# The last three expert down-projection slots and their epilogue moved two column halves later in TensorE's stream

## The chip, the cores and the metric

The kernel runs on one core of one Trainium2 chip. The metric is the device time of one execution in microseconds (us). Where it is on record, the mean clock that was granted to TensorE over the run stands beside the time, as a share of full speed.

## The reference, cut to what matters

```python
# x: 2048 x 1024, bf16
g = sigmoid((x * gate_w).sum(-1))
a = ssm(x)                                  # a scan over 2048 steps between two projections
idx = argsort(-(x @ w_r))[:8]               # 8 rows of x
y = (silu(x[idx] @ w_gate) * (x[idx] @ w_up)) @ w_down      # w_down: 3584 x 1024
b = x + scatter_add(idx, y * sigmoid(r[idx]))
out = g * a + (1 - g) * b
```

The long work on TensorE is the two projections of `a`. The expert part works on 8 rows only, but it has to read all of `w_gate`, `w_up` and `w_down` (22 MB in bf16).

## The kernel before

The kernel writes the instruction order of TensorE, VectorE, ScalarE and SyncE itself. The second projection ("S2", with H, the scanned states as VectorE prepares them, as one operand) goes through 16 row tiles `b`, each in two column halves `dh`. One half is 16 matmuls of 128x512. Other work is hung between the halves with `at((block, place), fn)`: it is issued after the first half whose place reaches it. In block 9 the halves are (12,0) at place 0.99, (12,1) at 1.99, (13,0) at 2.99 and (13,1) at 3.99.

Each expert step, a "slot", needs a weight tile of 8 KB per partition. Four tiles exist for the down-projection, and it has seven slots. A slot that has run gives its tile back, and the next load goes into it:

```python
def load_w():
    while nload[0] < NS and free_w:
        s = nload[0]
        tag = free_w.pop(0)
        ...                                     # w_gate, w_up slots cut
        w = const.tile([P, 2, 2, D], BF16, name="wd", tag=tag)
        for i in range(2):
            ...                                 # two items of 512 KB, nc.sync.dma_start(w[...], wd_v[...])
        wq[s] = (w, tag); nload[0] += 1

def moe_slot(s):
    for i in range(2):
        moe_item(2 * s + i, wq[s][0][:, i])     # down-projection: 8 narrow matmuls per item into y4 (PSUM)
    free_w.append(wq.pop(s)[1])
    load_w()
```

The epilogue turns `y4` into an update of 8 rows of the output. The last 256 rows of the output are read back after the scatter:

```python
def fin_a():        # ScalarE: 4 evictions of y4 to yc
def fin_b():        # VectorE: yc * rsel * (1 - g)
def scatter_upd():  # GpSimd: scatter-add of yc to out; SyncE: reload of the last rows, tile ul
...
at((9, 0.92), fin_a)
at((9, 0.1), lambda: last_m(1))
at((9, 0.95), lambda: (fin_b(), scatter_upd(), last_scan(1)))   # VectorE: fin_b ahead of the last scan
at((9, 2.5), lambda: fin(12))                                   # GpSimd: accumulating store of tile 12
at((9, 3.0), lambda: (last_post(1, 0, NCT // 2), last_post(1, NCT // 2, NCT)))   # H for tile 15
at((10, 0.5), lambda: (add_upd(NTT - 2), add_upd(NTT - 1)))     # VectorE: adds of ul
pos = [...] + [(8, 1.9)] * 4 + [(9, 0.9)] * 3                   # the seven down-projection slots at the end
```

## Time and profile before

| | before |
|---|---|
| time, median of 4 runs | 256.53 us (255.53 to 257.45) |
| span of the profiled run | 254.6 us |
| TensorE busy | 96% |
| granted clock of the profiled run | 0.985 |

The page of the profiled run gives the busy time of each engine (share of the span) and then the span in 40 slices, each digit a tenth of busy time; PEclk is the granted clock in tenths. TensorE is full except at the start, at the end and in two slices near the end (5 and 8), and the second of these has a low clock:

```profile
span 254.6 us, 3610 instructions
...
PE 244.9 (96%) x1414; PEld 116.0 (46%) x1414; DVE 227.1 (89%) x231; ACT 117.4 (46%) x203; POOL 33.5 (13%) x50
...
PE   7799999999999999999999999999999999589995
...
PEclk9999999999999999999999999999999999959999
```

The timeline of TensorE (start, length, line, shapes, count; in brackets how long it stood idle before and for what) shows that place. Line 672 is the down-projection, line 771 is S2, line 787 is the last row tile:

```profile
206.37 1.93 PE L672 MATMUL y<-wd,aT 128*32 128x256 bf16 x64
208.23 10.53 PE L771 MATMUL zps<-CT,H 128*128 128x512 bf16 x48
218.69 1.06 PE L672 MATMUL y<-wd,aT 128*32 128x256 bf16 x32
221.44 0.40 PE L672 MATMUL y<-wd,aT 128*32 128x256 bf16 x8 [1.68 <-DMA wd<-in_B_w_down_dram]
223.94 0.62 PE L672 MATMUL y<-wd,aT 128*32 128x256 bf16 x8 [2.10 <-DMA wd<-in_B_w_down_dram]
224.49 20.17 PE L771 MATMUL zps<-CT,H 128*128 128x512 bf16 x80
244.50 7.11 PE L787 MATMUL zps<-CT,H 128*128 128x512 bf16 x48
```

The first four slots (64 matmuls) run without a pause. The last three (48 matmuls) begin at 218.69 and are left at 224.49, with two pauses for a `wd` tile, 1.68 and 2.10 us. The next 80 matmuls take 20.17 us. The 48 ahead of the slots took 10.53 us.

In the list of waits of the last 50 us (engine, line and tile, what it waited for, then total, times and longest), these two pauses are the only waits of TensorE's matmuls, and the evictions of `y4` wait behind them:

```profile
ACT yc L691 <- PE y L672: 5.1, 1, 5.1
...
PE y L672 <- DMA wd<-in_B_w_down_dram: 3.8, 2, 2.1
```

The timeline of SyncE's queue shows why the tiles are late. The loads of the last three slots (7 pieces) are issued only from 207.03 on, as the first four slots (206.37 to 208.30) give their tiles back one by one:

```profile
207.03 5.00 SPq L641 DMA_DIRECT2D wd<-in_B_w_down_dram  x7
```

The windows view gives busy time, granted clock, DMA share and GB/s for stretches of 2 us:

```profile
core 0: us, PE busy (x), PEclk, DMA share, GB/s
218.00:220.00 2.00, 1.75 (x36) 1.00 1.05 399
220.00:222.00 2.00, 0.40 (x8) 1.00 1.08 273
222.00:224.00 2.00, 0.06 (x4) 0.81 0.08 17
224.00:226.00 2.00, 2.00 (x12) 0.50 0.00 0
...
228.00:230.00 2.00, 2.00 (x6) 0.50 0.00 0
230.00:232.00 2.00, 2.00 (x11) 0.99 0.00 0
```

DMA is full until 222 (share above 1, 273 to 399 GB/s). And the clock is 0.50 from the end of the pause on, although TensorE is busy again: a mean of 0.81 over 222 to 224 puts the fall at 224 - 2 * 0.19 / 0.5 = 223.2, and the 0.99 over 230 to 232 puts the rise at 230.0, so 6.8 us in all.

On VectorE the scaling of `yc` (line 696) stands ahead of the last scan (line 371) and of the multiplications that make H for tile 15 (line 383 and on):

```profile
227.76 0.23 DVE L365 TENSOR_TENSOR U<-U,cy 128x16 bf16<-128x16 bf16 x1
227.86 0.53 DVE L696 TENSOR_SCALAR yc<-yc,rsel_c,omg 8x1024 bf16<-8x1024 bf16 x1
228.31 4.46 DVE L371 TENSOR_TENSOR_SCAN U<-D,U 128x1024 bf16<-128x1024 f32 x2
232.80 0.69 DVE L383 TENSOR_TENSOR H<-U,Ctab 128x1024 bf16<-128x1024 bf16 x1
```

### The profile page before, as it was taken

The page shows a single profiled execution, that of the slowest core. Times are in us where ns is not written, and L with a number is a line of the kernel's source. Part 1 is how long each engine was busy: PE and PEld are TensorE (multiplying, and loading weights), DVE is VectorE, ACT ScalarE, POOL GpSimd, SP SyncE. Part 2 cuts the span into 40 slices and gives each one's busy share as a digit, 9 for nine tenths or more (in the row PEclk, how much of TensorE's full clock was granted, in tenths as well). Part 3 has the DMA queues.
Part 4 walks back from the last instruction along what each step waited for, and adds up shares of the span by engine and source line. Part 5 has one row for each costly group of instructions (what it writes and reads, how often), then busy time and mean ns, then how long its engine had stood idle before and what let it go on. Part 6 is the DMA issues. An engine that isn't in the chain of part 4 may idle for free.

```text
span 254.6 us, 3610 instructions
## 1 busy us (share of the span) xinstructions
PE 244.9 (96%) x1414; PEld 116.0 (46%) x1414; DVE 227.1 (89%) x231; ACT 117.4 (46%) x203; POOL 33.5 (13%) x50
## 2 busy tenths in 40 slices
PE   7799999999999999999999999999999999589995
PEld 5664444444444444444444444444444454324453
DVE  1899889999999999999899999999999999999412
ACT  3789973223516222542475432163484355135421
POOL 4000000000100003433220321001002110107200
PEclk9999999999999999999999999999999999959999
DMA  7999999999830000299969999584999829900811
GB/s 185 207 162 256 214 274 141 267 241 256 255 107 0 3 0 3 92 183 327 214 229 302 336 265 334 172 314 147 299 325 363 192 49 305 306 2 3 155 54 41
DMA packets 64193, 48.25 MB, mean 189 GB/s; under 512 B 49568, under 2 KB 51232, under 8 KB 64176
## 3 DMA queue, kind: packets, MB, share of 16 engines
q1 hardware_dynamic: 59120, 37.23, 54.5%
q0 software_dynamic: 3424, 7.90, 14.4%
q10 hardware_dynamic: 1632, 2.89, 3.3%
q8 instruction: 11, 0.18, 0.3%
q14 instruction: 6, 0.05, 0.1%
HBM read 27.55 MB, written 8.40 MB: 141 GB/s over the span
## 4 chain that ended last, share of the span: by engine, by line
PE 88%; DMA 8%; SPq 2%; DVE 0%; issue 0%
PE vps L266 41%; PE zps L771 38%; DMA wd<-in_B_w_down_dram 7%; PE zps L787 3%; PE pgu L660 3%; SPq L80 2%; DMA X<-in_A_x_dram 2%; PE vps L282 1%; PE zr L487 1%; PE y L672 0%; SPq L77 0%; DVE ot L792 0%; PE aT_ps L685 0%; PE xselT_ps L579 0%; PE zs_ps L595 0%
## 5 line engine op out<-in xcount | busy, mean ns | idle before, releaser
L771 PE MATMUL zps<-CT,H 128*128 128x512 bf16 x480 | 108.2, 386 | 0.0
L266 PE MATMUL vps<-X,BT 128*128 128x512 bf16 x480 | 105.1, 379 | 0.0
L771 PEld LDWEIGHTS <-H 128*128 128x128 bf16 x480 | 47.0, 99 | 58.4 <-issue 5.3
L266 PEld LDWEIGHTS <-BT 128*128 128x128 bf16 x480 | 46.4, 98 | 56.6 <-issue 0.8
L313 DVE TENSOR_TENSOR_SCAN U<-d,U 128x2048 bf16<-128x2048 f32 (+2 forms) x22 | 62.0, 2860 | 1.0 <-DVE U L304 0.5
L273 ACT CAST V<-vps 128x512 bf16<-128x512 f32 x60 | 32.2, 588 | 57.0 <-PE vps L266 57.0
L776 ACT ACTIVATE ot<-zps,gcol 128x512 bf16<-128x512 f32 x30 | 20.6, 687 | 56.1 <-PE zps L771 56.1
L302 DVE TENSOR_TENSOR U<-V,T2tab 128x4096 bf16<-128x4096 bf16 (+2 forms) x11 | 16.6, 1509 | 1.2 <-ACT V L273 0.8
L303 DVE TENSOR_TENSOR V<-V,nTi 128x4096 bf16<-128x4096 bf16 (+2 forms) x11 | 16.7, 1516 | 0.5
L304 DVE TENSOR_TENSOR U<-U,V 128x4096 bf16<-128x4096 bf16 (+2 forms) x11 | 16.7, 1516 | 0.4
L797 POOL DMA_DIRECT2D out_dram<-ot x14 | 12.9, 919 | 29.6 <-ACT ot L776 27.5
L338 DVE TENSOR_TENSOR U<-U,S2tab 128x4096 bf16<-128x4096 bf16 x7 | 16.0, 2292 | 0.2
L340 DVE TENSOR_TENSOR H<-H,U 128x4096 bf16<-128x4096 bf16 x7 | 16.0, 2292 | 0.2
L336 DVE TENSOR_TENSOR H<-U,Ctab 128x4096 bf16<-128x4096 bf16 x7 | 16.0, 2284 | 0.0
L745 ACT CAST zps<-xd 128x512 f32<-128x512 bf16 (+1 forms) x25 | 14.2, 575 | 3.2 <-ACT xt L732 3.0
L709 POOL DMA_DIRECT2D xt<-in_A_x_dram x12 | 7.1, 592 | 62.6 <-DMA out_dram<-xt 40.8
L732 ACT ACTIVATE xt<-xt,omgcol 128x1024 bf16<-128x1024 bf16 x12 | 13.7, 1145 | 0.0
L801 DVE TENSOR_TENSOR ot<-ot,xt 128x512 bf16<-128x512 bf16 x3 | 1.3, 426 | 9.5 <-ACT ot L776 4.8
L282 PE MATMUL vps<-X,BT 128*128 128x256 bf16 x64 | 7.3, 273 | 1.9 <-DMA BT<-in_A_B_re_dram 1.6
L727 DVE TENSOR_TENSOR xd<-xt,Dbc 128x1024 bf16<-128x1024 bf16 x12 | 7.8, 685 | 1.4 <-DMA xt<-in_A_x_dram 1.1
L371 DVE TENSOR_TENSOR_SCAN U<-D,U 128x1024 bf16<-128x1024 f32 x4 | 8.9, 2272 | 0.1
L672 PE MATMUL y<-wd,aT 128*32 128x256 bf16 x112 | 4.0, 283 | 3.8 <-DMA wd<-in_B_w_down_dram 3.8
(161 smaller groups left out, 159.8 us busy)
## 6 DMA issues: line engine op xcount, KB each, us to landing
wgu<-in_B_w_gate_dram SPq DMA_DIRECT2D x16, 448.0 KB, 6.4
wgu<-in_B_w_up_dram SPq DMA_DIRECT2D x16, 448.0 KB, 6.5
wd<-in_B_w_down_dram SPq DMA_DIRECT2D x12, 512.0 KB, 7.6
out_dram<-ot POOLq DMA_DIRECT2D x14, 256.0 KB, 5.7
xt<-in_A_x_dram POOLq DMA_DIRECT2D x12, 256.0 KB, 4.5
out_dram<-xt ACTq DMA_DIRECT2D x10, 256.0 KB, 4.9
xt<-in_A_x_dram SPq DMA_DIRECT2D x4, 256.0 KB, 3.4
out_dram<-xt POOLq DMA_DIRECT2D x4, 256.0 KB, 3.9
```

The source lines that it names most:

```text
L266: nc.tensor.matmul(o, lhsT=BT[pl][:, dc, ct * P:(ct + 1) * P], rhs=X[m][:, dc, k0 * LC:k1 * LC], start=(dc == 0), stop=(dc == KD - 1))
L273: nc.scalar.copy(out=V[k][:, :, ct, :], in_=vp[m, ct][:, :, kk, :])
L302: nc.vector.tensor_tensor(out=u, in0=v, in1=T2tab[:, :, c0:c1, :], op=ALU.mult)
L303: nc.vector.tensor_tensor(out=v, in0=v, in1=bc(nTi, c0, c1), op=ALU.mult)
L304: nc.vector.tensor_tensor(out=u, in0=u, in1=V[k][:, ::-1, c0:c1, :], op=ALU.add)
L313: nc.vector.tensor_tensor_scan(out=fl, data0=d0[:, c0:c1, :].rearrange("p c t -> p (c t)"), data1=fl, initial=0.0, op0=ALU.mult, op1=ALU.add)
L336: nc.vector.tensor_tensor(out=h, in0=g, in1=bc(Ctab, c0, c1), op=ALU.mult)
L338: nc.vector.tensor_tensor(out=g, in0=g, in1=S2tab[:, :, c0:c1, :], op=ALU.mult)
L340: nc.vector.tensor_tensor(out=h, in0=h, in1=G[k][:, ::-1, c0:c1, :], op=ALU.add)
L745: nc.scalar.copy(out=z[:], in_=xd[b][:, d_:d_ + w])
L771: nc.tensor.matmul(zps[:], lhsT=H[k][:, pl, ct, tl * P:(tl + 1) * P], rhs=CT[pl][:, ct, dsl], start=(fresh and ct == 0 and pl == 0), stop= ...
L776: nc.scalar.activation(out=ots[b][:, dsl], in_=zps[:], func=ACT.Copy, scale=gcol[:, b:b + 1])
```

## The change

The intent is to let the `wd` tiles land while TensorE does two more column halves, so that it finds them loaded. The slots move from behind (12,0) to behind (13,0), and the epilogue moves with them.

```diff
-    at((9, 0.92), fin_a)
+    at((9, 2.92), fin_a)
...
-    at((9, 0.95), lambda: (fin_b(), scatter_upd(), last_scan(1)))
+    at((9, 2.95), lambda: (fin_b(), scatter_upd(), last_scan(1)))
...
-    pos = [...] + [(8, 1.9)] * 4 + [(9, 0.9)] * 3
+    pos = [...] + [(8, 1.9)] * 4 + [(9, 2.9)] * 3
```

No computing or DMA instruction is added or taken away. VectorE and SyncE keep their order. On GpSimd the store of tile 12 comes ahead of the scatter; on ScalarE the evictions of `y4` come behind the evictions of (12,1) and (13,0).

More of the change, by code (lines that the diff above doesn't have):

```diff
@@ L892 @@
     at((10, 0.5), lambda: (add_upd(NTT - 2), add_upd(NTT - 1)))
-    pos = [(3, 4.9)] * 2 + [(4, 1.9)] * 3 + [(5, 1.9)] * 3 + [(6, 1.9)] * 3 + [(6, 5.9)] * 3 + [(7, 0.9)] * 2 + [(8, 1.9)] * 4 + [(9, 0.9)] * 3
+    pos = [(3, 4.9)] * 2 + [(4, 1.9)] * 3 + [(5, 1.9)] * 3 + [(6, 1.9)] * 3 + [(6, 5.9)] * 3 + [(7, 0.9)] * 2 + [(8, 1.9)] * 4 + [(9, 2.9)] * 3
     for s in range(NW // 2):
```

## The prediction

> **What bounds the kernel now.** TensorE: the page gives it 244.9 of a span of 254.6 us (96%), and the chain of waits is 88% TensorE. The exception sits near the end. The engine timeline shows TensorE meeting the last three down-projection slots (48 matmuls, line 672) at 218.69 and leaving them at 224.49. It stood still 1.68 and 2.10 us there, waiting for the w_down tiles. Their loads take over the four tiles that the first four slots give back at 206.4 to 208, so they cannot start sooner. The windows view shows DMA at a share near 1 and about 300 to 400 GB/s from 210 to 222, and the last tile releases TensorE at 223.94.
>
> The pause has a second price. The windows view gives a granted clock of 1.00 until 223, then 0.50 from about 223.6 to 230.4, then 1.00 again. The first column half after the pause took about 6.35 us (ScalarE evicts it at 230.88); the others take 3.45. [...]
>
> **What the change does.** No instruction is added or removed. On TensorE the 48 matmuls move behind column halves (12,1) and (13,0). On ScalarE the four evictions of y (1.49 us together) move behind the scaling of x tile 15. On GpSimd the accumulating store of output tile 12 now precedes the scatter, which also waits for it to land. VectorE keeps its order, but its scaling of y (0.53 us), which sits in front of the last scan, will wait for the later y.
>
> **Cost.** TensorE runs the two halves from 218.69 to 225.6. All w_down tiles landed by 223.9, 1.7 us earlier, and their loads are triggered as before. The 48 matmuls at the pace of the first 64 (1.86 us for 64) take 1.4 us.
> - Pause and slots: 5.8 us become 1.4, gain 4.4.
> - Halved clock: five column halves took 20.17 us and at 3.455 take 17.28, gain 2.9.
> Sum about 7.25 us, all on the TensorE chain. Tile 14 then ends at 237.4 instead of 244.5, and the last tile near 244.3.
>
> **Does something else catch up?** y ends at 227.05, ScalarE (tile 15 first) finishes yc at about 229.0, VectorE scales it by 229.5 instead of 228.4: the last scan slips 1.2 us. The first half of the last H is then ready at 236.1 (needed 237.4), the second at 238.1 (needed 240.9). Scatter from 229.9, landed 236.7; reload of the last rows usable at 240.1; two adds and two output halves done by 242.4, where the first eviction of tile 15 comes at about 243.3. Slack is about 1 us in both chains: tight, but nothing on the path.
>
> **Predicted time.** 256.5 - 7.25 = 249.3 us; 8 in 10 between 248.3 and 251.0. Chances: faster by over 2% 0.92, within 2% 0.07, slower by over 2% 0.01.
>
> **What would show it.** Waits of line 672 on w_down gone (3.8 us before); granted clock 1.00 from 220 on; column halves after the slots at 3.45 us each; a new wait of VectorE of about 1.2 us before the scaling of y; no wait of TensorE on H before the last tile; the last stores 7 us earlier.
>
> **What would make it wrong.** The w_down tiles landing later than 225.6, so that a short pause stays. The narrow matmuls or another gap still leading to a half-clock window: only the 4.4 us would come, near 252.1. The scatter waiting long for tile 12's store, or VectorE's slip over 1.3 us: then the reload or the last scan holds the last tile and up to 1 to 2 us go.

That the half clock belongs to the pause and goes with it was the author's estimate from one trace; experiments 2 and 3 test it. 4.4 us of pause and slots and 2.9 us of half clock make about 7.25 us.

## More of the kernel before

Before, VectorE does not wait at line 696: ScalarE has evicted `yc` by 226.1 (line 691, 224.60 to 226.09), and VectorE arrives there at 227.86.

## The result, and the profile after

| | before | after |
|---|---|---|
| time, median of 4 runs | 256.53 us (255.53 to 257.45) | 249.75 us (248.93 to 250.03) |
| span of the profiled run | 254.6 us | 248.3 us |
| TensorE busy | 96% | 98% |
| granted clock of the profiled run | 0.985 | 1.00 |

The ratio is 0.9731, with a 95% interval of 0.9688 to 0.9775: faster. A ratio here is the mean time of one kernel's fast runs over the mean of the other's fast runs of the same rounds, so it is not quite the ratio of the medians quoted. The time lies in the predicted range.

The page after; the gap and the slice of low clock are gone:

```profile
span 248.3 us, 3608 instructions
...
PE 242.7 (98%) x1414; PEld 115.6 (47%) x1414; DVE 227.0 (91%) x231; ACT 117.4 (47%) x203; POOL 33.6 (14%) x50
...
PE   7899999999999999999999999999999999999995
...
PEclk9999999999999999999999999999999999999999
```

TensorE's timeline after. Five halves run in a row (80 matmuls, 17.44 us), the 48 narrow matmuls take 1.49 us without a pause, and everything behind runs at the same pace:

```profile
207.09 1.93 PE L672 MATMUL y<-wd,aT 128*32 128x256 bf16 x64
208.95 17.44 PE L771 MATMUL zps<-CT,H 128*128 128x512 bf16 x80
226.32 1.49 PE L672 MATMUL y<-wd,aT 128*32 128x256 bf16 x48
227.75 10.53 PE L771 MATMUL zps<-CT,H 128*128 128x512 bf16 x48
238.12 7.11 PE L787 MATMUL zps<-CT,H 128*128 128x512 bf16 x48
```

Both profiles reach the first four slots at nearly the same time (206.37 and 207.09; the 0.72 us were lost earlier, in parts that the change does not touch). From there to the end it was 48.2 us before and is 41.2 us now, a gain of 7.0 us.

The windows after, in the same stretches and columns: TensorE full, clock 1.00.

```profile
220.00:222.00 2.00, 2.00 (x11) 1.00 1.08 341
222.00:224.00 2.00, 2.00 (x11) 1.00 0.43 82
224.00:226.00 2.00, 2.00 (x11) 1.00 0.47 34
226.00:228.00 2.00, 2.00 (x52) 1.00 0.58 100
```

The waits after have none for `wd`, and one new wait of VectorE for the evictions of `y4`, 2.6 us:

```profile
DVE yc L696 <- ACT yc L691: 2.6, 1, 2.6
```

VectorE after: line 696 starts at 229.56, and the two halves of H (line 385) are ready at 236.65 and 238.71. TensorE starts tile 15 at 238.12 and needs the second half of H only half a tile later, so it does not wait.

```profile
226.76 0.23 DVE L365 TENSOR_TENSOR U<-U,cy 128x16 bf16<-128x16 bf16 x1
229.56 0.53 DVE L696 TENSOR_SCALAR yc<-yc,rsel_c,omg 8x1024 bf16<-8x1024 bf16 x1 [2.57 <-ACT yc L691]
...
235.96 0.69 DVE L385 TENSOR_TENSOR H<-H,U 128x1024 bf16<-128x1024 bf16 x1
...
238.02 0.69 DVE L385 TENSOR_TENSOR H<-H,U 128x1024 bf16<-128x1024 bf16 x1
241.30 1.29 DVE L760 TENSOR_TENSOR xt<-xt,ul 128x1024 bf16<-128x1024 bf16 x2 [2.59 <-DMA ul<-out_dram]
242.51 0.75 DVE L801 TENSOR_TENSOR ot<-ot,xt 128x512 bf16<-128x512 bf16 x2
244.24 0.43 DVE L801 TENSOR_TENSOR ot<-ot,xt 128x512 bf16<-128x512 bf16 x1 [0.97 <-ACT ot L789]
```

### The profile page after: what moved, and what is told of

Its sections match the earlier page's. It is cut to its first block, busy times and chain, and to the rows that moved or that the text cites. A ratio compares the mean times of both kernels' runs of the same rounds, so it can differ in the third digit from the quotient of the medians.

```text
span 248.3 us, 3608 instructions
## 1 busy us (share of the span) xinstructions
PE 242.7 (98%) x1414; PEld 115.6 (47%) x1414; DVE 227.0 (91%) x231; ACT 117.4 (47%) x203; POOL 33.6 (14%) x50
## 4 chain that ended last, share of the span: by engine, by line
PE 84%; DVE 7%; DMA 4%; SPq 3%; issue 0%; ACT 0%; DVEq 0%
PE zps L771 42%; PE vps L266 32%; DMA X<-in_A_x_dram 4%; PE zps L787 3%; PE pgu L660 3%; SPq L80 2%; PE vps L282 1%; PE y L672 1%; DVE U L302 1%; DVE U L313 1%; DVE H L340 1%; DVE U L338 1%; DVE H L336 1%; PE zr L487 1%; DVE S2tab L252 1%; DVE Ctab L251 1%
## 5 line engine op out<-in xcount | busy, mean ns | idle before, releaser
L771 PE MATMUL zps<-CT,H 128*128 128x512 bf16 x480 | 105.5, 379 | 0.0
L266 PEld LDWEIGHTS <-BT 128*128 128x128 bf16 x480 | 46.4, 98 | 56.6 <-PE pgu L660 0.7
L771 PEld LDWEIGHTS <-H 128*128 128x128 bf16 x480 | 46.2, 98 | 56.3 <-issue 1.5
L282 PEld LDWEIGHTS <-BT 128*128 128x128 bf16 x64 | 6.1, 98 | 2.4 <-issue 0.7
L660 PE MATMUL pgu<-wgu,xsel 128*32 128x448 bf16 x128 | 7.2, 354 | 0.0
```

Source lines behind the costliest of these rows:

```text
L266: nc.tensor.matmul(o, lhsT=BT[pl][:, dc, ct * P:(ct + 1) * P], rhs=X[m][:, dc, k0 * LC:k1 * LC], start=(dc == 0), stop=(dc == KD - 1))
L282: nc.tensor.matmul(vps[:, pl, c, :], lhsT=BT[pl][:, dc, ct * P:(ct + 1) * P], rhs=X[0][:, dc, k * LC:(k + 1) * LC], start=(dc == 0), stop= ...
L771: nc.tensor.matmul(zps[:], lhsT=H[k][:, pl, ct, tl * P:(tl + 1) * P], rhs=CT[pl][:, ct, dsl], start=(fresh and ct == 0 and pl == 0), stop= ...
```

## The experiments

Each ran with a profile and five timed rounds. Runs of one call share the runs of before: experiments 2, 3, 5 and 7 are one call, 1, 4, 8 and 9 another, 6 and 10 the third. The kernel before ran 33 times, and its times fall into two groups by granted clock:

| before | runs | mean time |
|---|---|---|
| mean clock 0.992 to 0.993 | 20 | 255.38 us |
| mean clock 0.985 to 0.987 | 13 | 256.65 us |
| all | 33 | 255.88 us |

The trace of experiment 1, with a mean of 0.993, has one stretch at 0.50: its windows view gives 0.79 over 224 to 226, 0.50 over 226 to 228 and 0.86 over 228 to 230, so it went from about 225.16 to 228.56, 3.40 us; the 6.8 us above (6.83 in the clock record of the trace) are twice that. A clock of 0.50 for one stretch of 3.41 us lowers the mean over 254 us by 0.5 * 3.41 / 254 = 0.0067, and for two stretches by 0.0134. So, as an estimate from their means, the first group lost one such stretch and the second two. The profile that the prediction was made from (6.8 us at 0.50) belongs to the second group. Means of 0.997 to 0.999, which several changed kernels show, come from a lowered clock after the last matmul where a trace was looked at: the windows view of the run with only the last slot moved has 1.00 in every stretch asked for up to 248 and 0.57 over 248 to 250, where TensorE does nothing.

### 1. Only the epilogue later

The slots stay; `fin_a`, `fin_b`, scatter and last scan move.

```diff
-    at((9, 0.92), fin_a)
+    at((9, 2.92), fin_a)
-    at((9, 0.95), lambda: (fin_b(), scatter_upd(), last_scan(1)))
+    at((9, 2.95), lambda: (fin_b(), scatter_upd(), last_scan(1)))
```

> The slots stay where they were before; only the epilogue (evictions of y, scaling, scatter, reload, last scan) is issued two column halves later, as in the change. My theory: the place of the epilogue buys nothing, TensorE still waits about 4.4 us and loses one or two half-clock windows: same as before, about 255.7 us, granted clock 0.985 to 0.993 in every run. Rival (the new order of GpSimd and ScalarE brings the gain): about 250 us.

Measured: 255.68 us, ratio 1.001 (0.998 to 1.004); clock 0.993 in four runs and 0.987 in two. The timeline of TensorE has both pauses still:

```profile
221.59 0.40 PE L672 MATMUL y<-wd,aT 128*32 128x256 bf16 x8 [1.79 <-DMA wd<-in_B_w_down_dram]
224.09 0.40 PE L672 MATMUL y<-wd,aT 128*32 128x256 bf16 x8 [2.09 <-DMA wd<-in_B_w_down_dram]
224.42 12.22 PE L771 MATMUL zps<-CT,H 128*128 128x512 bf16 x48
```

So the new order on ScalarE and GpSimd brings nothing by itself. This profile fell in a run with one stretch of half clock, and its 48 matmuls behind the slots took 12.22 us, against 10.53 us at full clock.

### 2. The loads taken away, the slots left where they were

A wrong result: the last three slots use the tiles of three slots earlier.

```diff
+            if s >= NS - 3:
+                wq[s] = (kept[s - 3], None)      # no tile, no load
+                nload[0] += 1
+                continue
...                                              # cut: kept[s] = w; these slots give no tile back
```

> Wrong result on purpose: before, but the last three slots use tiles that are already loaded (those of three slots earlier), so no load of w_down stands behind them and 3 MB are not read. The slots stay where they were. My theory: the late w_down tiles alone make the pause, so it is gone and with it the half clock: about 249.3 us, as the change. Rival (the place of the slots, or what ScalarE, VectorE and GpSimd do around it, makes the difference): clearly over 250.5 us, up to 256.5 us.

Measured: 249.62 us, ratio 0.9764 (0.9727 to 0.9801), with no wait on `wd`. The 48 matmuls of the slots run without a pause:

```profile
219.12 1.49 PE L681 MATMUL y<-wd,aT 128*32 128x256 bf16 x48
```

This is the time of the change, with the slots in their old place. The late tiles are the cause of the pause. (The edit takes 3 MB of traffic away as well, but the list of waits of before has no other transfer that TensorE waited for here, and experiment 8 keeps the traffic.) (The kernel passed the comparison with the reference all the same, although it multiplies with wrong weights: the comparison does not see this error, which can reach 8 rows of 2048 at most. A pass says little about this part of the kernel.)

### 3. Both pauses filled with dummy matmuls

```diff
+            if s == NW // 2 - 1:
+                filler((8, 10)[i])       # 128x512 matmuls, result unused
             moe_item(2 * s + i, wq[s][0][:, i])
```

> Before, with 8 and 10 dummy matmuls (128x512, result unused, about 1.7 and 2.2 us at full clock) ahead of the two items of the last slot, where TensorE stood still 1.68 and 2.10 us. The slots stay where they were, so the w_down tiles are waited for as before. My theory (pause 4.4 us plus half clock 2.9 us): the useful work resumes as late as before, but the granted clock stays 1.00, so only the 2.9 us come: about 253.6 us. Rival A (the slow column half after the pause has another cause, for example the ScalarE eviction of y or DMA traffic): 256.5 us, first column half after the slots still about 6.3 us. Rival B (the halved clock counts for nothing, all gain is the pause): 256.5 us as well.

Measured: 253.88 us, ratio 0.9932 (0.9892 to 0.9972), clock 1.00 in all six runs. The timeline shows that the useful work still waits, now behind the dummies, and that the 80 matmuls behind take 17.44 us as in the change (the view counts 78, two records are missing):

```profile
219.78 1.90 PE L650 MATMUL fill<-CT 128*128 128x512 bf16 x7
221.61 0.40 PE L680 MATMUL y<-wd,aT 128*32 128x256 bf16 x8
221.95 2.33 PE L650 MATMUL fill<-CT 128*128 128x512 bf16 x10
224.21 0.40 PE L680 MATMUL y<-wd,aT 128*32 128x256 bf16 x8
224.54 17.44 PE L779 MATMUL zps<-CT,H 128*128 128x512 bf16 x78
```

From the first of these lines to the fourth is the old pause, 4.4 us, about 0.2 us longer than before. So the clock alone is worth about 255.88 - 253.86 = 2.0 us on average (means; against the runs of before of the same call it is 1.8 us, and the longer pause hides some 0.2 us of it), and rivals A and B fall.

### 4. Only the second pause filled

As experiment 3 with `filler((0, 10)[i])`.

> As before, but only the second wait is filled (10 dummy matmuls), the first of about 1.7 us stays. It tells what counts as idle for the clock. If only standing still counts, the pause is shorter than the 2.04 us of the run with the first wait filled, where 3 of 6 runs lost one window: at most that many runs below 1.00, about 254 to 254.8 us. If the narrow matmuls of the slots (128x32 weights) count little as well, there is a stretch of 1.06 + 1.68 + 0.40 = 3.1 us of low activity, longer than there (2.04 + 0.40 + 0.40 = 2.8 us): a clock of about 0.993 in more than half of the runs, about 255.3 us.

Measured: 253.60 us, ratio 0.9923 (0.9895 to 0.9951), clock 1.00 in all six runs. One pause of 1.77 us, in a stretch with narrow matmuls on both sides, did not lower the clock in any of these six runs.

### 5. Only the first pause filled

As experiment 3 with `filler((8, 0)[i])`; a pause of 2.04 us stays.

> As the run with both fills, but only the first wait is filled with 8 dummy matmuls; the second pause of about 2.1 us stays. [...] the clock stays 1.00 and the time is about 253.6 us. If any pause over about 2 us lowers the clock, it falls to 0.50 again and the time is about 256.5 us.

Measured: 255.23 us, ratio 0.9987 (0.9946 to 1.0028). Neither forecast holds: three runs are at 1.00 (254.08 to 255.28 us) and three at 0.993 (255.17 to 256.15 us), the mean clock of one stretch of half clock. So half of the runs with this single pause lost about what experiment 1 shows. The profile of this run, where the pause is 2.04 us, is one of those at 1.00; the three at 0.993 have no trace.

The clock does not change at the same places in all traces. The clock record in the trace of before has 1.00 from 4.77 us on for 218.45 us, 0.50 for 6.83 us, 1.00 for 23.89 us and then 0.50, after the last matmul; that of after has 1.00 from 6.29 us on for 242.35 us and then 0.50, also after the last matmul. These lengths are 64, 2, 7 and 71 times 3.413 us. Why it is so, no run here shows. The table gives TensorE's work in the stretches of 3.41 us around each fall (for experiment 1 estimated from its timeline and the 225.16 above):

| trace | stretch, us | TensorE busy in it | clock behind it |
|---|---|---|---|
| before | 219.81 to 223.22 | 0.40 us | falls to 0.50 |
| before | 223.22 to 226.63 | 2.69 us | stays at 0.50 |
| before | 226.63 to 230.05 | all of it | rises to 1.00 |
| experiment 1 | 218.34 to 221.75 | about 1.6 us | stays at 1.00 |
| experiment 1 | 221.75 to 225.16 | about 1.3 us | falls to 0.50 |
| experiment 1 | 225.16 to 228.56 | all of it | rises to 1.00 |

In before the pause ran on 0.7 us past the fall (223.22 to 223.94), and the clock stayed low for 6.83 us; in experiment 1 it had ended at 224.09, about 1.07 us ahead of the fall, and the clock stayed low for 3.40 us. That the one explains the other is argued from these two traces, not tested.

### 6. 144 narrow dummies in the changed kernel

```diff
+        if s == NW // 2 - 3:
+            narrow(144)                  # the slots' shape: 128x32 weights, 256 columns
```

> The change, with 144 dummy matmuls of the slots' own narrow shape (128x32 weights, 256 columns, result unused) right before the three slots, so 192 of them stand in a row without a pause, about 5.6 us. At the slots' pace (1.49 us for 48) the dummies cost about 4.3 us: about 254.0 us with a granted clock of 1.00 if narrow matmuls count as work for the clock. If they count as idle, [...] the clock falls to 0.50 in every run: over 255.5 us, mean clock 0.993 or less.

Measured: 253.85 us, ratio 0.9912 (0.9869 to 0.9954), clock 1.00 in five runs and 0.998 in one. The timeline has 4.11 us of dummies and 1.48 us of slots in a row, from 225.52 to 230.9 (the two overlap a little), and the windows view has 1.00 in each microsecond from 226 to 234. So about 5.4 us of narrow matmuls one behind the other did not lower the clock here; the falls in the traces of before and experiment 1 came where TensorE had stood still (1.68 and 2.10 us, 1.79 and 2.09 us).

### 7. One half later instead of two

```diff
-    pos = [...] + [(9, 0.9)] * 3         # and fin_a, fin_b at 1.92, 1.95
+    pos = [...] + [(9, 1.9)] * 3
```

> The three slots and their epilogue only one column half later instead of two. TensorE reaches them 3.45 us later than before and should wait only about 0.6 us in all for the last tile. My theory: pause shrinks from about 4.4 to about 0.6 us and the clock stays 1.00: about 249.8 to 250.3 us. Rival (the gain is proportional to how far the slots move, half of it for one half): about 253 us. Rival (only the pause matters, the half clock stays): about 252.7 us.

Measured: 250.43 us, ratio 0.9804 (0.9764 to 0.9845). TensorE waits once:

```profile
222.31 1.27 PE L672 MATMUL y<-wd,aT 128*32 128x256 bf16 x40
224.10 0.40 PE L672 MATMUL y<-wd,aT 128*32 128x256 bf16 x8 [0.52 <-DMA wd<-in_B_w_down_dram]
```

Half of the move brings nearly all of the gain, since the pause goes and the clock with it. Five of six runs are at 0.998 or above; one is at 0.993 with 251.63 us. That run has no trace here, and where it lost its clock stays open.

### 8. Only the last slot later

```diff
-    pos = [...] + [(9, 0.9)] * 3
+    pos = [...] + [(9, 0.9)] * 2 + [(9, 2.9)]     # fin_a, fin_b as in the change
```

> Two of the three slots stay where they were; only the last one, whose tile lands last, goes two column halves later, with the epilogue. My theory: the first two slots never waited (32 matmuls in 1.06 us), so this alone brings all of it: same time as the change, about 249.7 us, no wait on w_down, clock 1.00. Rival (all three slots have to move, because moving them relieves the loads): over 251.5 us.

Measured: 249.72 us, ratio 0.9765 (0.9736 to 0.9793), no wait on `wd`. The first two slots did not have to move. This is as fast as the change, not faster.

### 9. Three halves later

The slots at `(9, 3.9)`, `fin_a` and `fin_b` at 3.92 and 3.95, `last_post` behind them at 3.96.

> The three slots and the epilogue three column halves later than before, one more than in the change (the last multiplications of VectorE stay behind the last scan). TensorE has nothing to wait for at the slots. My theory: the slack behind the slots is only about 1 us, so y, VectorE's last scan behind it and the scatter and reload come about 2.5 us too late: VectorE's H holds TensorE 1 to 2 us before the last tile or the reload holds the last stores: about 251.5 to 252.5 us. Rival (later is free as long as TensorE has work): 249.7 us.

Measured: 251.84 us, ratio 0.9858 (0.9827 to 0.9889). The slots find their tiles, but TensorE now stands still in front of tile 15:

```profile
230.71 7.08 PE L771 MATMUL zps<-CT,H 128*128 128x512 bf16 x32
239.51 7.12 PE L787 MATMUL zps<-CT,H 128*128 128x512 bf16 x48 [1.72 <-DVE H L385]
```

The wait is for H: VectorE sat idle 4.20 us for `yc` ahead of the last scan. One half more than in the change is past the slack. The reload has no slack left either: VectorE waited 2.48 us for `ul` and began its adds at 243.99, from where it works to its end without a further wait, so the chain that ended last in this trace goes back over the reload to the scatter.

### 10. The change again

> The change itself once more, with more rounds, for the size of the gain against the runs of before of the same rounds. The runs of before at a mean clock of about 0.993 have lost one window of 3.41 us at half clock (1.7 us), those at about 0.986 two (3.4 us). So my 2.9 us for the clock was read from a profile of the dearer kind; with about six in ten runs of before at one window the mean loss is about 2.2 us, and the gain about 4.4 + 2.2 less the slip of other things, 5.8 to 6.4 us: ratio about 0.976. If 2.9 us holds: gain over 7 us, ratio under 0.973.

Measured: 249.35 us (249.04 to 250.51), ratio 0.9733 (0.9695 to 0.9772); clock 0.999 or 1.00 in all six runs. The runs of before were slower (mean 256.41 us), five of eleven of them with two stretches of half clock. The ratio forecast from the 22 runs of before that were known by then, 0.976, lies inside the interval, and so does 0.973, so this run does not tell the two apart. The gain in means was 256.41 - 249.49 = 6.9 us here, and 6.9 us in the first comparison too: above the forecast of 5.8 to 6.4 us and below 7 us.

No version beat the change. In its profile TensorE's timeline shows no wait from 11.93 us, when it starts the last part of the first projection tile, to 245.2 us.

## Why the prediction was right

The time was 249.75 us for a forecast of 249.3 us, and the mechanism held. Point by point:

- **The late tiles make the pause.** Shown: without the loads the old order is as fast as the change (experiment 2), and moving only the slot that waits is enough (experiment 8).
- **The pause, forecast 4.4 us.** The kernels that keep the pause and keep the clock (experiments 3 and 4) have means of 253.86 and 253.65 us, the change in experiment 10 one of 249.49 us. The middle of the first two less the third is 4.3 us (the pause of the filled kernels is some 0.2 us longer).
- **The half clock, forecast 2.9 us.** This term was too large for the average run. Before at 255.88 us less 253.75 us is 2.1 us. It is 1.6 us in the 20 runs with one stretch of half clock and 2.9 us in the 13 runs with two. The forecast came from one profile, and that one had two. So the sum is about 6.4 us on average over the 33 runs, not 7.25. The change gained 6.9 us. In experiment 10, five of the eleven runs of before had two stretches; for the first comparison the clocks are not on record, but three of its four runs of before (256.52 to 257.45 us) have times as in the group with two. The forecast time came out close in part by luck: it was 256.5 less 7.25 us, and that base was mostly such runs as well. Against a base of runs with one stretch, 255.4 us, the same sum would have given 248.1 us, below the stated range. The loss differs from run to run with the same code (20 runs of before at a mean clock of 0.992 to 0.993, 13 at 0.985 to 0.987), and the prediction did not use that for its range.
- **What else slips.** The forecast was 1.2 us of new wait on VectorE; it was 2.57 us. The scaling of `yc` started 1.7 us later than before (229.56 for 227.86), of which 0.72 us are the later start of this profile, and VectorE had got there 1.0 us earlier (226.99 for 227.99), so it waited longer. For H only the later start counts.
- **The slack, forecast about 1 us in both chains.** The first half of H was ready 1.5 us before TensorE came to tile 15 (236.65 and 238.12). The output halves of tile 14 were done at 243.26, and VectorE then sat idle 0.97 us until tile 15's first eviction. Experiment 9 shows that the slack is finite: one half later (3.45 us), TensorE waits 1.72 us for H and the time is 2.4 us above the change (means of different calls; 2.1 us above experiment 8 of the same call).
- **Matmuls at full pace.** 17.44 us for the five halves ahead of the slots and 10.53 us for three behind them, as forecast.

What stays open: what exactly lowers the clock. In these traces the fall came behind stretches of 3.41 us with 0.40 and about 1.3 us of work and not behind one with about 1.6 us. All 33 runs of before, with pauses of 1.68 and 2.10 us in the one profile of it, have a mean clock of 0.993 or less; with a single pause of 1.77 us none of six runs has, with one of 2.04 us three of six. No run here shows the rule behind these cases. What lifts the clock again is open too: behind a stretch with 2.69 us of work at half clock it stayed at 0.50.

## What to carry to other kernels

A load that goes into a buffer freed by the work just before it came late here (the 7 pieces issued from 207.03 on landed 4.6 to 12.2 us after their issue, and the last released TensorE at 223.94): put as much other work of the bound engine between as the load takes, and move only the piece that waits. The pause of TensorE cost more than its length here: behind it the clock was 0.50 for 6.83 us in the trace of before and for 3.40 us in that of experiment 1, and the runs that kept the pause without the half clock were about 2 us faster on average. Look at the granted clock of every run and not of the profiled run alone before such a loss is put into a sum. Work in the order of an engine has followers: what was moved here sits in front of VectorE's last scan, and one step further it gives back about a third of the gain (2.1 to 2.4 us of 6.4 to 6.9 us).
